# Seven block products in a feed-forward network: all factors of w_in made during the experts, longer load runs, conversion and activation steps staggered

## Chip, cores and metric

The kernel runs on one core of one Trainium2 chip. The metric is the time of one execution on the device in microseconds (us); lower is better.

## The reference

Attention with a threshold, then a mixture of eight experts (each token goes to the one expert with the highest logit), then a feed-forward network with a leaky activation. Only the last two stages are touched:

```
# x: 2304 tokens x 512; e runs over 8 experts, F = 1024
h = np.maximum(x[mask] @ w1[e], 0.0)
out[mask] = gate_w[mask, None] * (h @ w2[e])
# network: w_in 512 x 2048, w_out 2048 x 512, alpha 2048
h = x @ w_in
g = np.maximum(h, 0.0) + alpha * np.minimum(h, 0.0)
return (g @ w_out).astype(np.float32)
```

`w_in` and `w_out` arrive as 64-bit floats. The kernel takes them as pairs of 32-bit words and converts them on the chip.

## The kernel before

Every matrix product is made from operands split into a high half (rounded to fp32r) and a low half (what is left), with three matmuls: high by high, high by low, low by high. ScalarE (ACT) makes the high half, VectorE (DVE) or GpSimd (POOL) subtracts to get the low one. The order of instructions on each engine is the order in which the Python code issues them; every engine runs its own in that order and waits on semaphores. SyncE (SP) issues nearly all DMAs, also in order.

**Experts** (`experts`, L1050 to L1515). 64 steps `g`, eight for each expert `r = g // 8`. In a step, `l1` makes one 128-row piece of the hidden layer (12 matmuls on L1196, as wide as the expert's capacity: 432, 256, 384, 256, 368, 272, 320, 288 tokens), `relu` splits it (L1179, L1180), and `l2` multiplies the piece before by w2 (12 matmuls, L1227 to L1229). `wsplit` prepares a piece of w1 three steps ahead and a piece of w2 two steps ahead: a cast on ACT (L1108), a subtraction on DVE (L1109). Their loads (`wload`, L1095) bring 512 KB for two steps, in a ring of two; those of w1 are cut into 256 columns, so each run in memory is 1 KB.

Beside that, the steps carry other work. `conv` (L1555) turns one piece of w_in into fp32: ACT L1567, DVE L1569, L1571, L1573, L1584, L1585, POOL L1588; one conversion in 3.6 steps. From step 24 on, one entry of the list `early` is taken in each step: for w_in's row blocks 1, 2 and 0, `sums` (L1616: four additions, L1621 to L1624) and seven times `weights` (L1628: cast L1635, subtraction L1636, store L1637 to a DRAM buffer `ws`). From step 31 on, 18 scattered stores of the gate table go out on POOL (L1350). In the last expert, `ahead` fetches the network's first 768 tokens and makes differences and halves of them (`fetch`, `diff`, `split`, L1639 to L1671).

**Network** (`near_network`). Three passes `q` of 768 tokens, each of eight blocks `i` of 256 columns of w_in. Within a block, the first product is not made in eight quarter products but in seven, from sums and differences of the quarters of w_in and of the tokens: `prod` (6 matmuls of 128x384, L1724) in the order 1, 2, 6, 7, 5, 3, 4, into two PSUM banks `ha` and `hb`. `held` copies `ha` out on ACT (L1729). `act` adds it to `hb` on DVE (L1735), makes the two ReLU parts on ACT (L1742, L1743) and joins them on DVE (L1744) in pass 0, or does both on DVE (L1739, L1740) later, and then splits: `gh` on ACT (L1746), `gl` on POOL (L1747). `f2mm` (9 matmuls of 128x512, L1761 to L1763) multiplies by w_out; there are four in a block. So a block has 42 + 36 matmuls on TensorE (PE), the same in each pass.

Pass 0 also converts the fifteen remaining pieces of w_out (`conv` again, with POOL L1591 and L1592), one step of the generator after each product, and makes the factors of w_in's blocks 3 to 7 (`sums` on DVE, `weights` on DVE for two products and on POOL for five). Passes 1 and 2 load the factors from `ws` (L1632). At the end of a pass, `after` prepares the tokens of the next one (`diff` and `split` on DVE).

The program has a second branch for badly spread routing; it is not run here.

Of the kernel before, what the change touches and what calls it, by code (L numbers as in the profile page):

```python
# [44 lines left out]
CVG = {False: [18 * i // 5 for i in range(KF2 + 1)], True: [4 * i for i in range(15)] + [59, 61]}  # L45
# [6 lines left out]
NPRE = 3  # L52
EARLY = 24
AHEAD = 8 * (NE - 1)
# [157 lines left out]
def attn_moe_ffn(ctx: ExitStack, tc, q, k, v, tau, emb, mtau, w1, w2, w_in, w_out, alpha, out):  # L212
# [841 lines left out]
    def experts(CAPS, general, y2):  # L1054
# [7 lines left out]
        sm_p = mpool("sm", bufs=1)  # L1062
        stg_p = mpool("stg", bufs=2)
# [16 lines left out]
        def wload(which, u):  # L1080
# [6 lines left out]
            e = W[r]["e"]  # L1087
            t = stg_p.tile([128, 1024], F32, tag=f"stg{which}", name=f"stg{which}")
# [9 lines left out]
        def wsplit(which, g):  # L1098
# [3 lines left out]
            t = w_p.tile([128, 2, 512], F32R, tag=f"w{which}", name=f"w{which}")  # L1102
            if which == 1:
# [5 lines left out]
            nc.vector.tensor_tensor(t[:, 1], src, t[:, 0].bitcast(F32), op=ALU.subtract)  # L1109
# [378 lines left out]
        for g in range(NE * KF + 1):  # L1488
# [21 lines left out]
            if g >= AHEAD and ahead:  # L1510
                ahead.pop(0)(xt_p)
            if g >= EARLY and early:
                early.pop(0)()
# [10 lines left out]
    def shared(st, general):  # L1524

        y2 = {}
        aw_p = st.enter_context(tc.tile_pool(name="aw", bufs=KF2 if general else NP, side="right", reuse_waits="tile"))
        if general:
            WI = [aw_p.tile([128, 2, DM], F32R, tag="aw", name=f"wi{c}") for c in range(KF2)]
        else:  # L1530
            WA = [aw_p.tile([128, 2, DM], F32, tag="aw", name=f"wa{c}") for c in range(NP)]
# [12 lines left out]
        def cvload():  # L1544
# [5 lines left out]
            if which == 1:  # L1550
                nc.sync.dma_start(flat.rearrange("p (k f) -> p k f", k=KD),
                                  w_in.bitcast(U32)[:, c * 256:(c + 1) * 256].rearrange("(k p) f -> p k f", p=128))
            else:
                nc.sync.dma_start(flat, w_out.bitcast(U32)[c * 128:(c + 1) * 128, :])
            CV[which, c] = flat.rearrange("p (n w) -> p n w", w=2)  # L1555

        def conv():
# [19 lines left out]
            sums = which == 1 and not general  # L1577
            if not sums:
                if c not in WO:
                    WO[c] = aw_p.tile([128, 2, DM], F32R, tag="aw", name=f"wo{c}")  # L1580
                hl = WI[c] if which == 1 else WO[c]
                nc.scalar.copy(hl[:, 0, :], ff)
            yield
# [3 lines left out]
            if sums:  # L1587
                nc.gpsimd.tensor_tensor(WA[c // 2][:, c % 2], ff, rf, op=ALU.add)  # L1588
                yield
                return  # L1590
            nc.gpsimd.tensor_tensor(ff, ff, hl[:, 0, :].bitcast(F32), op=ALU.subtract)  # L1591
            nc.gpsimd.tensor_tensor(hl[:, 1, :], ff, rf, op=ALU.add)  # L1592
            yield
# [430 lines left out]
```

## Time and profile before

| | us |
|---|---|
| median of 3 runs (1078.19 to 1078.75) | 1078.25 |
| the profiled execution | 1081.63 |
| its span, first to last instruction | 1079.8 |
| PE busy, whole span | 984.6 (91%) |
| DVE, ACT, POOL busy | 767.9, 596.3, 587.4 |
| attention and routing | 0 to 358.4 |
| experts | 358.4 to 615.7 |
| network, pass 0 | 615.7 to 796.8 |
| network, pass 1 | 796.8 to 930.3 |
| network, pass 2 and the end | 930.3 to 1079.8 |

The stage limits are the starts of the first matmul of the stage on PE. PE's busy time is modelled at its ends, so it counts short gaps as busy; a stage's length against that of an undisturbed stretch with the same matmuls says more.

### The profile page before, as it was taken

The page shows a single profiled execution, that of the slowest core. Times are in us where ns is not written, and L with a number is a line of the kernel's source. Part 1 is how long each engine was busy: PE and PEld are TensorE (multiplying, and loading weights), DVE is VectorE, ACT ScalarE, POOL GpSimd, SP SyncE. Part 2 cuts the span into 40 slices and gives each one's busy share as a digit, 9 for nine tenths or more (in the row PEclk, how much of TensorE's full clock was granted, in tenths as well). Part 3 has the DMA queues.
Part 4 walks back from the last instruction along what each step waited for, and adds up shares of the span by engine and source line. Part 5 has one row for each costly group of instructions (what it writes and reads, how often), then busy time and mean ns, then how long its engine had stood idle before and what let it go on. Part 6 is the DMA issues. An engine that isn't in the chain of part 4 may idle for free. (4 is left out here: it accounts for less than half of the span.)

```text
span 1079.8 us, 18205 instructions
## 1 busy us (share of the span) xinstructions
PE 984.6 (91%) x6099; PEld 906.2 (84%) x6099; DVE 767.9 (71%) x1474; ACT 596.3 (55%) x1373; POOL 587.4 (54%) x592
## 2 busy tenths in 40 slices
PE   7999999999996999989979768877789999999995
PEld 6999998999996899989979767756678899888994
DVE  7999999999997777798768657766665344644342
ACT  6899898899995455455545354545453222322221
POOL 6989899899995111247631445556534232242233
PEclk8999999999997999999999878898889999999998
DMA  3333547335432858699997354333255344444321
GB/s 91 103 85 90 146 137 237 98 106 155 122 103 100 286 188 263 204 252 242 259 265 224 79 142 137 116 118 126 98 167 173 118 117 142 142 164 118 116 81 62
DMA packets 123015, 161.26 MB, mean 149 GB/s; under 512 B 23304, under 2 KB 80648, under 8 KB 122912
## 3 DMA queue, kind: packets, MB, share of 16 engines
q1 hardware_dynamic: 119312, 150.42, 47.6%
q0 software_dynamic: 3456, 9.46, 2.3%
q8 instruction: 50, 0.82, 0.3%
q14 instruction: 53, 0.43, 0.1%
q10 hardware_dynamic: 144, 0.13, 0.0%
HBM read 108.08 MB, written 43.04 MB: 140 GB/s over the span
## 5 line engine op out<-in xcount | busy, mean ns | idle before, releaser
L1747 POOL TENSOR_TENSOR gl<-c,gh 128x384 fp32r<-128x384 f32 x96 | 102.3, 1067 | 244.3 <-ACT gh L1746 224.9
L1724 PE MATMUL ha<-x,wr 128*128 128x384 f32 x576 | 122.7, 349 | 18.7 <-ACT v L1729 12.4
L1746 ACT CAST gh<-c 128x384 fp32r<-128x384 f32 x96 | 49.3, 513 | 157.5 <-DVE c L1740 122.0
L1724 PEld LDWEIGHTS ha<-x,wr 128*128 128x128 f32 x576 | 105.9, 194 | 31.3 <-ACT v L1729 15.5
L443 POOL TENSOR_TENSOR ptl<-x,pth 128x512 fp32r<-128x512 f32 x97 | 124.8, 1288 | 6.8
L1724 PE MATMUL hb<-x,wr 128*128 128x384 f32 x432 | 97.0, 362 | 27.4 <-DVE c L1735 25.0
L647 DVE SCALAR_TENSOR_TENSOR p<-s,mx,e 128x576 f32<-128x576 f32 x144 | 116.6, 812 | 6.8 <-ACT mx L635 2.9
L1196 PE MATMUL l<-x,w 128*128 128x256 f32 (+6 forms) x744 | 120.0, 310 | 0.0
L1109 DVE TENSOR_TENSOR w<-stg,w 128x512 fp32r<-128x512 f32 x128 | 104.1, 828 | 21.0 <-ACT w L1108 20.3
L1762 PE MATMUL o<-wo,gh 128*128 128x512 f32 x288 | 117.5, 408 | 0.0
L1763 PE MATMUL o<-wo,gl 128*128 128x512 f32 x288 | 116.8, 405 | 0.0
L1761 PE MATMUL o<-wo,gh 128*128 128x512 f32 x288 | 116.5, 405 | 0.0
L631 DVE TENSOR_REDUCE mx<-s 128x1 f32<-128x576 f32 x144 | 108.5, 754 | 8.6 <-PE s L624 5.5
L660 PE MATMUL t<-ident,p 128*128 128x128 f32 (+1 forms) x720 | 112.0, 277 | 2.2 <-ACT x L686 0.9
L1196 PEld LDWEIGHTS l<-x,w 128*128 128x128 f32 x744 | 112.0, 190 | 0.6
L1724 PEld LDWEIGHTS hb<-x,wr 128*128 128x128 f32 x432 | 82.1, 204 | 34.1 <-DVE c L1735 30.5
L640 ACT ACTIVATE e<-s,mx 128x576 f32<-128x576 f32 x144 | 106.3, 739 | 6.6 <-DVE mx L631 6.0
L1588 POOL TENSOR_TENSOR wa<-f,r 128x512 f32<-128x512 f32 x16 | 23.6, 1472 | 137.2 <-DVE r L1585 113.0
L1108 ACT CAST w<-stg 128x512 fp32r<-128x512 f32 x128 | 76.3, 619 | 38.6 <-DMA stg<-in_moe_w_dram 38.6
L1228 PE MATMUL y<-h,w 128*128 128x256 f32 (+6 forms) x256 | 80.7, 315 | 8.7 <-DVE h L1180 8.7
L660 PEld LDWEIGHTS t<-ident,p 128*128 128x128 f32 (+1 forms) x720 | 81.1, 137 | 8.0 <-ACT x L686 2.2
L1227 PE MATMUL y<-h,w 128*128 128x256 f32 (+6 forms) x256 | 82.8, 324 | 5.0 <-ACT yT L1235 3.5
(254 smaller groups left out, 2486.8 us busy)
## 6 DMA issues: line engine op xcount, KB each, us to landing
stg<-in_moe_w_dram SPq DMA_DIRECT2D x64, 512.0 KB
wr<-ws SPq DMA_DIRECT2D x126, 256.0 KB
ws<-wr SPq DMA_DIRECT2D x56, 256.0 KB
kx<-ks SPq DMA_DIRECT2D x60, 144.0 KB
xd<-zt SPq DMA_DIRECT2D x33, 256.0 KB
raw<-in_moe_w_in_dram SPq DMA_DIRECT2D x16, 512.0 KB
raw<-in_moe_w_out_dram SPq DMA_DIRECT2D x16, 512.0 KB
yd<-zt SPq DMA_DIRECT2D x19, 256.0 KB
```

The source lines that it names most:

```text
L443: lambda: nc.gpsimd.tensor_tensor(lo, raw, hi.bitcast(F32), op=ALU.subtract))
L631: nc.vector.tensor_reduce(out=mx[:, 0:1], in_=st["s", t][:, :, 0:288], op=ALU.min, axis=AX.XY)
L640: nc.scalar.activation(e, st["s", t][:, :, 0:288], AF.Exp, bias=st["mx", t][:, 0:1], scale=-1.0)
L647: nc.vector.scalar_tensor_tensor(out=p.rearrange("q (a b) -> q a b", a=2), in0=st["s", t][:, :, 0:288], scalar=st["mx", t][:, 2:3], in1=st ...
L660: nc.tensor.transpose(m[0:w, j * n + i * 128:j * n + (i + 1) * 128], st["p", t][:, c * 128:c * 128 + w], ident)
L1109: nc.vector.tensor_tensor(t[:, 1], src, t[:, 0].bitcast(F32), op=ALU.subtract)
L1196: nc.tensor.matmul(m[:, 0:n], w[:, a, c], st["x"][:, b, c, 0:n], start=(i == 0), stop=(i + 1 == len(terms)))
L1724: nc.tensor.matmul(m, w[:, a, k], x[:, b, k], start=start and n == 0, stop=n + 1 == len(terms), skip_group_check=not start)
L1747: nc.gpsimd.tensor_tensor(gl, c, gh.bitcast(F32), op=ALU.subtract)
L1761: nc.tensor.matmul(m, gh[:, ts], WO[f][:, 0, :], start=(n[0] == 1), stop=False)
L1762: nc.tensor.matmul(m, gh[:, ts], WO[f][:, 1, :], start=False, stop=False)
L1763: nc.tensor.matmul(m, gl[:, ts], WO[f][:, 0, :], start=False, stop=(n[0] == KF2))
```

## The change

1. All 56 factors (eight blocks by seven products) and the eight groups of sums are made during the experts, from step 6.8 on, all on POOL with the cast on ACT, and all are stored to `ws`. Pass 0 loads them from there as passes 1 and 2 do. The converted w_in is now kept for two blocks at a time.
2. w1 is loaded in pieces of 512 columns (1 MB for four steps, a ring of two), w_in in 512 words by 256 rows: runs of 2 KB in memory.
3. From step 7 on, every fourth piece of w2 has its low half made on POOL and not on DVE.
4. In the network, the steps after a product are put off: `join` comes one product later than the ReLU parts, `halves` one later still (`tick`); the generator of a conversion starts every fourth product and several run at once (`cstep`), with the cast a product after the DVE steps and POOL a product after that.
5. In the last expert, the tokens of five of the seven products (1, 2, 6, 7, 5) are split before the network begins, in its last four steps; before, it was three (1, 2, 6). At the end of a pass, differences 1 and 3 go to POOL, and half 6 is made after the addition of product 4, not before it.

```diff
-CVG = {False: [18 * i // 5 for i in range(KF2 + 1)], True: [4 * i for i in range(15)] + [59, 61]}
+CVG = {False: [17 * i // 5 for i in range(KF2 + 1)], True: [4 * i for i in range(15)] + [59, 61]}
...
-NPRE = 3
-EARLY = 24
-AHEAD = 8 * (NE - 1)
+AHEAD = {0: 0, 4: 1, 5: 2, 6: 3, 7: 4}
...
+            if which == 1 and not general:
+                a, b = ((0, 256), (256, 512))[u] if u < 2 else (0, 512)
+                if c % 2 == 0:
+                    STG[1, u] = stg_p.tile([128, KD, 512], F32, tag="stg1", name="stg1")
+                elif u > 1:
+                    return
+                f0 = c // 2 * 512
+                nc.sync.dma_start(STG[1, u - c % 2][:, :, a:b],
+                                  w1[bass.ds(e, 1), :, f0 + a:f0 + b].rearrange("o (k p) f -> p (o k) f", p=128))
+                return
...
+            eng = nc.gpsimd if not general and which == 2 and g % 4 == 1 and g > 8 else nc.vector
...
-            if g >= EARLY and early:
-                early.pop(0)()
+            while early and early[0][0] <= g:
+                early.pop(0)[1]()
...
+        def factor(i, p, eng):
+
+            t, flat, home = wtile(i, p)
+            src = SUM[i][p]
+            hi, lo = (t[:, x].rearrange("p (k j) -> p k j", k=2) for x in range(2))
+            nc.scalar.copy(hi, src)
+            eng.tensor_tensor(lo, src, hi.bitcast(F32), op=ALU.subtract)
             nc.sync.dma_start(home, flat)
+
+        def weights(q, i, p):
+
+            WT[q, i, p], flat, home = wtile(i, p)
+            nc.sync.dma_start(flat, home)
...
-        for i in (*range(1, NPRE), 0):
-            y2["early"] += [lambda i=i: sums(i, nc.gpsimd)] + [lambda i=i, p=p: weights(0, i, p, nc.gpsimd, True) for p in PROD]
+        G = nc.gpsimd
+        for i in range(NP):
+            g0 = 6.8 * i + 6.8
+            y2["early"].append((g0, lambda i=i: sums(i, G)))
+            y2["early"] += [(g0 + 0.8 * x, lambda i=i, p=p: factor(i, p, G)) for x, p in enumerate(PROD)]
+        y2["early"] += [(61.5 + 0.3 * x, lambda p=p: weights(0, 0, p)) for x, p in enumerate(PROD)]
...
+        def tick():
+            for x in pend:
+                x.pop(0)()
+            pend[:] = [x for x in pend if x] + fresh
+            fresh.clear()
...
+        def cstep():
+
+            if count[0] % 4 == 0 and count[1] < KF2 - 1:
+                live.append(conv())
+                count[1] += 1
+            count[0] += 1
+            for x in list(live):
+                if next(x, 1):
+                    live.remove(x)
...
-                for f, x in {6: [(split, 1)], 7: [(split, 2)], 5: [(diff, 1), (diff, 3)], 3: [(diff, 2), (split, 6)],
-                             4: [(diff, 4)]}.get(p, ()):
-                    f(x, V)
+                for f, x, e in {6: [(split, 1, V)], 7: [(split, 2, V)], 5: [(diff, 1, P)], 3: [(diff, 2, V), (diff, 3, P)],
+                                4: [(split, 6, V), (diff, 4, V)]}.get(p, ()):
+                    f(x, e)
...
-                if q == 0 and NPRE <= i + 1 < NP:
-                    sums(i + 1, V)
...
-                def step(p, m, start=False):
-                    prod(q, i, p, m, start)
-                    next(stages, None)
+                def step(p):
+                    tick()
+                    after(q, i, p)
+                    cstep()
```

POOL during the experts, about step 36 before the change, rows that only repeat left out here and below (`wa` is a converted piece of w_in, `sum` the sums, `wr` a factor, `pd` the gate table):

```order
L1588 TENSOR_TENSOR wa_5885<-f,r 128x512
L1636 TENSOR_TENSOR wr<-wa_5883,wr 128x256
L1350 DMA pd<-idg,ysl_i 2304x2
L1636 TENSOR_TENSOR wr<-sum,wr 128x256
L1588 TENSOR_TENSOR wa_5886<-f,r 128x512
```

and after it, between two conversions at about step 13:

```order
L1611 TENSOR_TENSOR wa<-f,r 128x512
L1646 TENSOR_TENSOR sum<-wa 128x256
L1647 TENSOR_TENSOR sum<-sum,wa 128x256
L1648 TENSOR_TENSOR sum<-wa 128x256
L1649 TENSOR_TENSOR sum<-wa,sum 128x256
L1662 TENSOR_TENSOR wr<-wa,wr 128x256
L1133 TENSOR_TENSOR w_6771<-stg_6574,w_6771 128x512
L1662 TENSOR_TENSOR wr<-sum,wr 128x256 x3
L1611 TENSOR_TENSOR wa<-f,r 128x512
```

The sums, the factors and the low half of a w2 piece (L1133) now stand together on POOL, all through the experts.

POOL in pass 0, in a middle block, before (`gl` is the low half of the activation, `wo` a piece of w_out):

```order
L1747 TENSOR_TENSOR gl<-c,gh 128x384
L1636 TENSOR_TENSOR wr<-wa_5886,wr 128x256
L1636 TENSOR_TENSOR wr<-sum,wr 128x256
L1591 TENSOR_TENSOR f<-f,wo_9939 128x512
L1592 TENSOR_TENSOR wo_9939<-f,r 128x512
```

and after:

```order
L1790 TENSOR_TENSOR gl<-c,gh 128x384 x2
L1616 TENSOR_TENSOR f<-f,wo_9271 128x512
L1617 TENSOR_TENSOR wo_9271<-f,r 128x512
L1790 TENSOR_TENSOR gl<-c,gh 128x384
L1616 TENSOR_TENSOR f<-f,wo_9272 128x512
```

The factors are gone from it; only activations and conversions are left.

ACT in pass 0, from the first copy of a block on, before (`v`, `w`, `d` are copies of `ha`, `u` and `c` the ReLU parts):

```order
L1729 COPY v<-ha 128x384
L1635 CAST wr<-wa_5888 128x256
L1742 ACTIVATE u<-c 128x384
L1743 ACTIVATE c<-c 128x384
L1746 CAST gh<-c 128x384
L1567 ACTIVATE f<-raw 128x512
L1729 COPY w<-ha 128x384
L1582 CAST wo_10313<-f 128x512
L1729 COPY d<-ha 128x384
```

and after:

```order
L1764 COPY v<-ha 128x384
L1789 CAST gh<-c 128x384
L1777 ACTIVATE u<-c 128x384
L1778 ACTIVATE c<-c 128x384
L1614 CAST wo_9277<-f 128x512
L1764 COPY w<-ha 128x384
L1594 ACTIVATE f<-raw 128x512
L1764 COPY d<-ha 128x384
```

Before, the cast `gh` stood right behind the ReLU parts that it needs joined on DVE; now the cast behind the first copy belongs to an earlier product.

## Rows read from the trace of the kernel before

**Rows 1.** Busy time by stage: stretch, length, five engines, PE clock, DMA share, GB/s.

```profile
core 0: us, PE busy (x) PEld busy (x) DVE busy (x) ACT busy (x) POOL busy (x), PEclk, DMA share, GB/s
358.40:615.70 257.30, 243.64 (x1613) 236.33 (x1614) 199.54 (x339) 132.45 (x292) 93.06 (x76) 0.99 0.80 226
615.70:796.80 181.10, 142.62 (x599) 120.47 (x599) 121.01 (x165) 87.11 (x188) 101.71 (x87) 0.87 0.42 136
796.80:930.30 133.50, 128.96 (x625) 114.98 (x623) 63.11 (x103) 36.68 (x70) 39.82 (x38) 0.97 0.44 133
```

**Rows 2.** The same view, by blocks of the network.

```profile
635.90:655.90 20.00, 17.42 (x80) 15.42 (x79) 13.43 (x17) 9.31 (x20) 10.20 (x8) 0.91 0.37 131
655.90:775.50 119.60, 94.83 (x391) 79.09 (x390) 81.75 (x115) 56.97 (x128) 71.03 (x63) 0.87 0.34 117
775.50:796.80 21.30, 17.72 (x80) 14.87 (x79) 13.80 (x19) 10.37 (x21) 11.98 (x10) 0.92 0.62 209
796.80:820.60 23.80, 19.26 (x80) 16.30 (x79) 16.03 (x24) 11.26 (x19) 10.02 (x10) 0.86 0.37 117
820.60:836.30 15.70, 15.70 (x80) 14.11 (x79) 6.07 (x12) 3.49 (x7) 5.53 (x6) 1.00 0.48 158
930.30:951.60 21.30, 18.16 (x80) 15.47 (x80) 14.86 (x23) 10.11 (x17) 9.94 (x10) 0.92 0.43 138
```

**Rows 3.** Who waited for whom in pass 0, 615.7 to 796.8: total us, times, longest.

```profile
ACT gh L1746 <- DVE c L1744: 33.0, 30, 2.9
PE hb L1724 <- DVE c L1735: 19.8, 13, 3.2
PE ha L1724 <- ACT v L1729: 12.4, 5, 4.4
```

**Rows 4.** Timeline, single operations: start, length in us, engine, line, operation.

```profile
628.14 1.26 POOL L1591 TENSOR_TENSOR f<-f,wo 128x512 f32<-128x512 f32 x1
629.47 1.27 POOL L1592 TENSOR_TENSOR wo<-f,r 128x512 fp32r<-128x512 f32 x1
788.73 1.02 POOL L1747 TENSOR_TENSOR gl<-c,gh 128x384 fp32r<-128x384 f32 x1 [1.04 <-ACT gh L1746]
632.43 0.42 DVE L1569 TENSOR_SCALAR f<-f 128x512 f32<-128x512 f32 x1
548.65 0.69 DVE L1573 SCALAR_TENSOR_TENSOR f<-raw,f 128x512 uint32<-128x512 uint32 x1
631.90 0.62 DVE L1744 SCALAR_TENSOR_TENSOR c<-u,na,c 128x384 f32<-128x384 f32 x1 [1.15 <-ACT c L1743]
```

**Rows 5.** Timeline, the same DVE subtraction alone and beside POOL.

```profile
539.66 0.69 DVE L1109 TENSOR_TENSOR w<-stg,w 128x512 fp32r<-128x512 f32 x1 [0.31 <-ACT w L1108]
...
597.82 2.18 POOL L1665 TENSOR_TENSOR raw<-raw 128x768 f32<-128x768 f32 x1
598.22 2.33 DVE L1109 TENSOR_TENSOR w<-stg,w 128x512 fp32r<-128x512 f32 x1
```

**Rows 6.** Busy time by stretches of the experts, columns as in the first group.

```profile
395.20:420.10 24.90, 24.90 (x206) 24.78 (x205) 22.63 (x43) 15.51 (x35) 3.02 (x2) 1.00 0.79 250
516.40:544.40 28.00, 27.29 (x206) 26.13 (x204) 22.42 (x35) 15.25 (x36) 20.70 (x19) 1.00 1.05 252
544.40:581.30 36.90, 31.05 (x206) 29.48 (x205) 25.16 (x44) 18.57 (x41) 6.99 (x6) 1.00 0.91 251
...
534.00:544.00 10.00, 10.00 (x78) 9.53 (x77) 8.57 (x15) 4.23 (x10) 6.65 (x6) 1.00 1.12 206
```

**Rows 7.** POOL's groups during the experts: busy us, mean ns, idle before.

```profile
L1588 POOL TENSOR_TENSOR wa<-f,r 128x512 f32<-128x512 f32 x16 | 23.6, 1472 | 137.2 <-DVE r L1585 113.0 <-ACT h L1179 20.8 <-DMA ws<-wr 3.4
L1350 POOL DMA_INDIRECT pd<-idg,ysl_i x18 | 21.7, 1204 | 2.9 <-issue 2.4 <-DMA ws<-wr 0.2
L1636 POOL TENSOR_TENSOR wr<-sum,wr 128x256 fp32r<-128x256 f32 x12 | 11.5, 960 | 6.7 <-ACT wr L1635 6.7
L1623 POOL TENSOR_TENSOR sum<-wa 128x256 f32<-128x256 f32 x3 | 2.9, 967 | 0.0
```

More of the change, by code (lines that the diff above doesn't have):

```diff
@@ L1062, in experts @@
         sm_p = mpool("sm", bufs=1)
+        if not general:
+            y2["wa"] = mpool("wa", bufs=1)
         stg_p = mpool("stg", bufs=2)
@@ L1102, in wsplit @@
             t = w_p.tile([128, 2, 512], F32R, tag=f"w{which}", name=f"w{which}")
+            eng = nc.gpsimd if not general and which == 2 and g % 4 == 1 and g > 8 else nc.vector
+            if which == 1 and not general:
+                t = t.rearrange("p x (k f) -> p x k f", k=KD)
+                v, j = u // 2 * 2, g % 4
+                src = STG[1, v][:, :, j * 128:(j + 1) * 128]
+                nc.scalar.copy(t[:, 0], src)
+                nc.vector.tensor_tensor(t[:, 1], src, t[:, 0].bitcast(F32), op=ALU.subtract)
+                RING[which, g] = t
+                if g == 1:
+                    wload(1, 2)
+                elif j == 3:
+                    STG.pop((1, v))
+                    wload(1, v + 4)
+                return
             if which == 1:
@@ L1586, in conv @@
             cvload()
-            if sums:
+            yield
+            if which == 1 and not general:
+                if c % 2 == 0:
+                    WA[c // 2] = y2["wa"].tile([128, 2, DM], F32, tag="wa", name="wa", bufs=2)
                 nc.gpsimd.tensor_tensor(WA[c // 2][:, c % 2], ff, rf, op=ALU.add)
-                yield
                 return
+            hl = WI[c] if which == 1 else WO[c]
+            nc.scalar.copy(hl[:, 0, :], ff)
+            yield
             nc.gpsimd.tensor_tensor(ff, ff, hl[:, 0, :].bitcast(F32), op=ALU.subtract)
             nc.gpsimd.tensor_tensor(hl[:, 1, :], ff, rf, op=ALU.add)
-            yield
         y2["cvload"], y2["conv"] = cvload, conv
@@ L1625, in sums @@
[L1625 to L1633 removed]
+            s = y2["wa"].tile([128, 4, 256], F32, tag="sum", name="sum", bufs=1)
@@ L1712, in near_network @@
         NQ = NT // NB
-        sums, weights, fetch, split, diff = (y2[x] for x in ("sums", "weights", "fetch", "split", "diff"))
+        weights, fetch, split, diff = (y2[x] for x in ("weights", "fetch", "split", "diff"))
         conv, cvload, rawtile = y2["conv"], y2["cvload"], y2["rawtile"]
```

146 lines of the change are left out of this document (75 added, 71 removed).

## The prediction

> **What bounds the kernel now.** I read the busy times by stage first. The chain that ended last is no help here: it holds only the final scatters. In the experts PE is busy 243.6 of 257.3 us, in pass 0 only 142.6 of 181.1, in pass 1 129.0 of 133.5 [rows 1]. All passes have the same matmuls, so the blocks of the network show what pass 0 could be: an undisturbed block takes 15.7 us at a granted clock of 1.00 [rows 2], eight of them 125.6 us. Pass 0 has 55 us more than that. The reader should see three levels in [rows 2]: 15.7 us with PE alone; 20.0 us in the second block, which has conversions of w_out but makes no factors; and 119.6 us for the five blocks after it, 23.9 each, where factors are made too. The first blocks of passes 1 and 2 stand out as well, with 23.8 and 21.3. Last, the waits of pass 0 [rows 3]: PE waits 19.8 us for DVE's addition to free `hb` and 12.4 us for ACT's copy of `ha`, and ACT waits 33.0 us, in 30 pieces, for DVE's join before it can cast `gh`. So PE is held up by engines that are themselves stuck behind a step of the same product. The granted clock of 0.86 to 0.91 there is a mixture of the two levels, 1.2 and 2.4 GHz, that follows PE's gaps.
>
> The experts are nearer to a bound. Where steps are short (256 tokens), a stretch without POOL work takes 24.9 us for eight steps with DVE busy 22.6; the stretch with 272 tokens, POOL busy 20.7 and DVE 22.4 takes 28.0 where the same pace per column would give 26.5 (24.9 x 272 / 256); and in the one of 320 tokens, 36.9 us, PE is busy 31.1 only, behind a stretch where the DMA share was 1.12 with 206 GB/s [rows 6].
>
> **Term 1, factors leave pass 0: -19.6 us.** Blocks 3 to 7 lose sums, casts, subtractions and stores, and become like block 2: 119.6 - 5 x 20.0 = 19.6 [rows 2]. What replaces them is a load of 256 KB per product, as passes 1 and 2 have it without a loss (158 GB/s at a share of 0.48 in the 15.7 us block).
>
> **Term 2, staggered steps: -20 us.** What is left is at most 20.0 - 15.7 = 4.3 us a block, at least nothing. An operation that reads two tiles of SBUF on DVE and one on POOL do not run at once: the subtraction on L1109 takes 0.69 us alone and 2.33 us when it starts in the middle of a POOL operation, which itself runs 2.18 us [rows 5]. So I add up what excludes each other in a block after the change: on POOL four `gl` of 1.02 and two conversions of 1.26 + 1.27, 9.1 us; on DVE four joins of 0.62 and two conversions of 0.42, 0.43 (the next of the same kind) and 0.69, 5.6 us [rows 4]. That is 14.7 us in a block that PE can do in 15.7: it does not bind by itself, but leaves little room. I take six tenths of the 4.3 us as gained, so 17.4 us a block, because the waits that hold PE are those that the new order pulls apart: 19.8 + 12.4 us [rows 3] of the 38.5 in which PE is idle. The first block keeps two token splits (18.5 us where 181.1 - 20.0 - 119.6 - 21.3 = 20.2 were), the last keeps the next pass's (18.7 where 21.3 were). Pass 0 becomes 18.5 + 6 x 17.4 + 18.7 = 141.6 us, 39.5 less than now; 19.6 of it is term 1.
>
> The Trainium skill states this exclusion too (SBUF — State Buffer, section Who interferes with whom): VectorE and GpSimd share a pair of ports, whoever issues first has it for the whole instruction, and the other is blocked, not slowed. The trace agrees, with 2.33 us for 0.69. A rule that speaks against the change stands in Perfetto Trace Analysis, section Optimizing Scalar/DVE Operations, of the same skill: as the two share that port, moving operations between them might not help. By that rule the fourteen w2 halves given to POOL cost more exclusive time than they save, and the third case below becomes likelier; the rows do not show the moved operation.
>
> **Term 3, ends of passes: -3.5 us.** The two first blocks have 8.1 and 5.6 us over 15.7 [rows 2]. In both, DVE's addition for product 4 stands behind difference 2 and split 6; the split now comes after it, but difference 2 waits for difference 1, which is now made on the slower POOL. Bounds: a small loss of 2 us and a gain of 8; I take 3.5, a quarter of the excess, since the splits themselves stay.
>
> **Term 4, experts: +10 us.** Moved in: five more sums of four operations and 32 more factors on POOL, 14 w2 halves on POOL instead of DVE, 39 more transfers of 256 KB on SP's queue (32 stores, 7 loads at the end). POOL's new work at the means of [rows 7]: 20 x 0.97 + 32 x 0.96 + 14 x 1.47 (as L1588, same size) = 71 us, on top of 93.1 [rows 1], so 164 of 257. Before, 113.0 us of POOL's time went in waiting for DVE's conversion [rows 7], so POOL has room on average. What counts is the short experts, where PE does not cover it. The 256-token stretch without POOL work should become like the 272-token one: 24.9 to 28 us. The 272-token stretch has the gate stores (18 of 1.20 us, most of them there) beside more factors: +2.5 us. The others, longer or already loaded, +1 together. DMA: 226 GB/s over 257.3 us are 58.1 MB [rows 1]; 39 x 0.26 MB and one early piece of w_out (0.5 MB) make 68.8. The 516 to 544 stretch moved 252 GB/s at a share of 1.05, so about 240 at full share; the 256-token one 250 at 0.79, so 316 [rows 6]. At those, 68.8 MB need 287 or 218 us: between them lies the length of the stage, and loads will come late at times. Against that stand the longer runs (the 15.7 us block with 2 KB runs alone gives 158 / 0.48 = 329 GB/s, 4% over 316) and w1 loaded a step of 1 MB ahead. I add 3.5 us for late loads. Sum 3.1 + 2.5 + 1 + 3.5 = 10. Every factor store makes SP wait for POOL, and the loads of w2 queue behind it; that is in these 3.5 us. Bounds: nothing lost, or +30 (all 68.8 MB at 240 GB/s, 287 us).
>
> The new splits in the last expert, two more on DVE and one on POOL, fall in its last steps, which have no w1 pieces left to prepare; I cost them at nothing, and 2 us more if DVE's `h` waits behind them.
>
> **Sum:** -39.5 - 3.5 + 10 = -33. The profiled execution's own 1081.6 would become 1048.6; the median of the runs is 3.4 us lower, so I forecast 1078.3 - 33 = **1045 us**.
>
> **Rivals.**
> First, forecast: 1045, its own range 1033 to 1058. Chance 0.52.
> Second, PE bound: the stagger takes all of it. Pass 0 is 8 x 15.7 + 4 us for the splits = 130, -51; the ends give 5, the experts lose 2 because w1's longer lead pays for the stores. 1078.3 - 54 = 1024. For it: 14.7 us of exclusive work is less than 15.7. Against: each engine runs in order, and 94% filled without a gap is rare. Chance 0.17.
> Third, the stagger does not do what it says: POOL and DVE exclude each other as before, a block stays at 20.0 us, the ends give nothing, the experts +10: 1078.3 - 19.6 + 10 = 1069, and to 1085 where w2 pieces come late on POOL. For it: the block of 20.0 us has exclusive work of 14.7 us already, so order, not amount, must give the rest. Against: 33.0 us of ACT waiting that the new order removes. Chance 0.20.
> Fourth, slower: the DMA queue binds the experts. If 68.8 MB go at the 206 GB/s of the stretch with a share of 1.12 [rows 6], where stores of yT and factors met, the stage lasts 334 us, +77, and the total is 1078 - 43 + 77 = 1112. It decides from a rate below 229 GB/s (68.8 MB in 257.3 + 43 us). For it: 2.3 times as many factor stores. Against: the stretch lasted 10 us, and longer ones held 251. Chance 0.11.
>
> **How the numbers follow.** About 0.2% (2 us) is what a measurement of this kernel can tell from no change. The first two cases are faster. Of the third, 0.14 is faster, 0.04 within that bound, 0.02 slower; of the fourth, 0.10 slower and 0.01 the same. So faster 0.83, same 0.05, slower 0.12. The range goes from 1018 (which leaves out 0.02 of the second case) to 1070 (which leaves out the upper third of the third, 0.07, and the fourth, 0.11).
>
> **What would show it.** Pass 0 should be near 142 us with middle blocks of 17 to 18 us and a clock over 0.9; ACT's wait for the join should fall from 33.0 us to under 10. The experts should last near 267 us, longer in the short experts than now, with POOL over 150 us busy. The first blocks of passes 1 and 2 should lose 1 to 3 us each; the others stay at 15.7. I am wrong if middle blocks stay at 20 (term 2), if the experts grow by over 25 us (term 4), or if DMA waits appear in pass 0.

## Result and profile after

| | before | after |
|---|---|---|
| median, us | 1078.5 (4 runs, 1078.2 to 1081.0) | 1050.7 (4 runs, 1048.4 to 1056.5) |
| profiled execution, us | 1081.6 | 1048.4 |
| experts | 257.3 | 267.1 |
| network, pass 0 | 181.1 | 143.8 |
| network, pass 1 | 133.5 | 130.9 |
| network, pass 2 and the end | 149.5 | 146.3 |

The ratio of the times is 0.9745, with a 95% interval of 0.9703 to 0.9788. The medians are 27.8 us apart, and the interval gives 23 to 32 us. The profiled executions are 33.2 us apart, against a forecast of 33; but the one after is the fastest of its four, and the one before took longer than all four in the table. So the stage lengths, which come from these two executions, overstate the gain by about 5 us in all.

Busy time by stage after the change (columns as in [rows 1]):

```profile
358.40:625.50 267.10, 249.50 (x1612) 241.92 (x1613) 207.63 (x325) 143.87 (x329) 162.65 (x146) 0.96 0.88 258
625.50:769.30 143.80, 128.21 (x599) 112.17 (x598) 104.58 (x135) 72.66 (x150) 81.33 (x62) 0.95 0.54 169
769.30:900.20 130.90, 128.10 (x625) 114.20 (x624) 65.64 (x100) 35.97 (x71) 45.48 (x42) 0.99 0.45 137
```

Set against [rows 1], the experts are 9.8 us longer and POOL works 162.7 us in them, not 93.1. Pass 0 is 37.3 us shorter; the same 599 matmuls keep PE busy 128.2 us instead of 142.6, because the clock is at its higher level for more of the time (granted clock 0.95, was 0.87), and the rest of the gain is waiting that is gone.

The same view for some blocks of the network after the change, to be read beside [rows 2]: blocks 2, 5 and 6 of pass 0, the first blocks of passes 1 and 2.

```profile
658.60:674.30 15.70, 15.70 (x80) 14.12 (x79) 12.34 (x18) 9.29 (x20) 10.42 (x8) 1.00 0.55 185
708.80:730.80 22.00, 18.78 (x80) 16.42 (x78) 14.11 (x17) 10.17 (x22) 9.55 (x8) 0.84 0.45 159
730.80:749.30 18.50, 16.20 (x79) 14.04 (x78) 14.29 (x17) 8.72 (x19) 10.04 (x8) 1.00 0.43 141
769.30:790.30 21.00, 18.20 (x79) 15.30 (x78) 15.23 (x23) 11.36 (x20) 10.85 (x10) 0.92 0.43 136
900.20:917.90 17.70, 16.12 (x79) 13.96 (x79) 15.02 (x23) 9.51 (x16) 9.38 (x9) 1.00 0.50 160
```

Pass 0 is uneven: its blocks take 15.5, 17.6, 15.7, 16.9, 17.6, 22.0, 18.5 and 20.0 us. Block 2 runs at PE's own pace with conversions beside it; the last three are furthest from it. The first blocks of the later passes are 2.8 and 3.6 us shorter.

Who waited for whom in pass 0 after the change (total us, times, longest; rows of [rows 3] are the counterparts):

```profile
ACT u L1777 <- DVE c L1773: 41.0, 21, 5.7
...
PE hb L1759 <- DVE c L1773: 11.2, 6, 3.2
...
ACT gh L1789 <- DVE c L1785: 4.4, 2, 2.2
```

ACT's wait for the join fell from 33.0 to 4.4 us, and PE's wait for the addition from 19.8 to 11.2. ACT now waits for that addition instead, 41.0 us. Most of this is idle time and costs nothing; the longest pieces, of over 5 us, are where PE waits too.

Busy time in the experts 1, 3, 5 and 7 (256, 256, 272 and 288 tokens) after the change:

```profile
395.20:420.10 24.90, 24.90 (x205) 24.77 (x205) 23.30 (x37) 15.95 (x37) 16.91 (x15) 1.00 0.79 270
...
454.20:480.20 26.00, 24.88 (x205) 24.68 (x205) 24.58 (x45) 15.40 (x36) 16.69 (x18) 1.00 1.00 265
...
518.30:550.80 32.50, 29.93 (x206) 28.78 (x206) 25.40 (x37) 17.64 (x42) 25.99 (x25) 0.89 1.01 252
...
586.70:625.50 38.80, 31.33 (x206) 30.20 (x205) 19.51 (x25) 16.88 (x38) 26.62 (x20) 0.87 0.67 194
```

The short expert 1 takes 24.9 us as before [rows 6], now with 16.9 us of POOL work in it where there were 3.0. The losses are late: expert 4 (38.1 us, was 34.1), 5 (32.5, was 28.0) and 7 (38.8, was 34.3). What ended waits in the experts after the change:

```profile
ACT w L1132 <- DMA stg<-in_moe_w_dram: 40.2, 15, 9.2
DVE h L1204 <- ACT h L1203: 29.5, 28, 2.6
DVE w L1133 <- ACT w L1132: 15.4, 5, 9.0
```

The first of these before the change, for the loads of w1 and w2 together:

```profile
ACT w L1108 <- DMA stg<-in_moe_w_dram: 31.5, 19, 4.0
```

ACT stands 40.2 us at the cast of a w2 piece whose load has not landed, once for 9.2 us in the last expert. The ReLU of a step is queued behind that cast on ACT, and PE waits for the ReLU. Loads were late before the change too (31.5 us), but in shorter pieces.

### The profile page after: what moved, and what is told of

Same layout as the page of the kernel before. It is cut to its first block, busy times and chain, and to the rows that moved or that the text cites. A ratio compares the mean times of both kernels' runs of the same rounds, so it can differ in the third digit from the quotient of the medians.

```text
span 1046.5 us, 18304 instructions
## 1 busy us (share of the span) xinstructions
PE 972.2 (93%) x6099; PEld 900.1 (86%) x6099; DVE 765.9 (73%) x1426; ACT 590.6 (56%) x1373; POOL 642.4 (61%) x640
## 4 chain that ended last, share of the span: by engine, by line
PE 53%; DVE 16%; issue 8%; DMA 8%; ACT 7%; POOL 7%; SPq 0%; POOLq 0%; ACTq 0%; DVEq 0%
PE ha L1759 7%; PE hb L1759 6%; PE s L622 5%; PE o L1819 5%; PE o L1818 5%; PE o L1817 5%; PE t L658 4%; DMA stg<-in_moe_w_dram 4%; PE l L1220 4%; DVE p L645 2%; DVE mx L629 2%; PE v L702 2%; PE m L721 2%; PE v L703 2%; PE y L1252 2%
## 5 line engine op out<-in xcount | busy, mean ns | idle before, releaser
L1790 POOL TENSOR_TENSOR gl<-c,gh 128x384 fp32r<-128x384 f32 x96 | 106.7, 1114 | 221.6 <-ACT gh L1789 134.2
L1759 PE MATMUL ha<-x,wr 128*128 128x384 f32 x576 | 118.4, 341 | 4.4 <-ACT c L1778 2.8
L1818 PE MATMUL o<-wo,gh 128*128 128x512 f32 x288 | 115.2, 400 | 0.0
L1817 PE MATMUL o<-wo,gh 128*128 128x512 f32 x288 | 114.1, 396 | 0.0
L1759 PE MATMUL hb<-x,wr 128*128 128x384 f32 x432 | 91.1, 347 | 15.3 <-DVE c L1773 15.3
L1251 PE MATMUL y<-h,w 128*128 128x256 f32 (+6 forms) x256 | 84.9, 332 | 11.2 <-ACT h L1203 7.3
L1759 PEld LDWEIGHTS hb<-x,wr 128*128 128x128 f32 x432 | 78.3, 194 | 18.7 <-DVE c L1773 18.1
L1252 PE MATMUL y<-h,w 128*128 128x256 f32 (+6 forms) x256 | 82.7, 323 | 6.4 <-DVE h L1204 6.2
L622 PE MATMUL s<-ks,qs 128*128 128x288 f32 x256 | 82.7, 338 | 2.9 <-ACT qs L529 1.4
L1253 PE MATMUL y<-h,w 128*128 128x256 f32 (+6 forms) x256 | 81.5, 318 | 0.0
L1773 DVE TENSOR_TENSOR c<-hb,d 128x384 f32<-128x384 f32 x24 | 13.4, 557 | 91.4 <-ACT d L1764 91.4
```

What stands on the lines that cost most here:

```text
L622: nc.tensor.matmul(s[:, hf, 0:288], lt, st[nm, a][:, hf * 288:(hf + 1) * 288], start=(j == 0 and x == 0), stop=(j == n - 1 and x == 1))
L1759: nc.tensor.matmul(m, w[:, a, k], x[:, b, k], start=start and n == 0, stop=n + 1 == len(terms), skip_group_check=not start)
L1790: nc.gpsimd.tensor_tensor(gl, c, gh.bitcast(F32), op=ALU.subtract)
L1817: nc.tensor.matmul(m, gh[:, ts], WO[f][:, 0, :], start=(n[0] == 1), stop=False)
L1818: nc.tensor.matmul(m, gh[:, ts], WO[f][:, 1, :], start=False, stop=False)
```

## Experiments

Times are medians; the ratio is to the kernel before, run on the same chip. Stage lengths are those of each kernel's profiled execution.

| kernel | us | ratio, 95% interval | experts | pass 0 |
|---|---|---|---|---|
| changed kernel | 1050.7 | 0.9745 [0.9703, 0.9788] | 267.1 | 143.8 |
| activation at once | 1076.2 | 0.9967 [0.9947, 0.9986] | 263.9 | 162.9 |
| before, activation staggered | 1056.1 | 0.9778 [0.9754, 0.9802] | 252.5 | 163.2 |
| w2 on DVE | 1053.1 | 0.9737 [0.9700, 0.9774] | 268.1 | 145.6 |
| each store twice | 1195.7 | 1.1045 [1.1013, 1.1078] | 413.2 | 144.2 |
| copy to a second buffer | 1072.8 | 0.9933 [0.9905, 0.9962] | 293.9 | 141.5 |
| w1 in halves, 1 KB runs | 1046.7 | 0.9686 [0.9663, 0.9710] | 265.2 | 142.2 |
| third buffer for w2 | 1035.2 | 0.9581 [0.9562, 0.9599] | 254.2 | 142.2 |
| third buffer, other splits | 1037.4 | 0.9604 [0.9574, 0.9633] | 251.5 | 144.6 |
| old order of a conversion | 1037.6 | 0.9596 [0.9567, 0.9625] | 269.2 | 131.1 |
| POOL's pair earlier | 1039.6 | 0.9607 [0.9574, 0.9640] | 270.7 | 133.6 |
| third buffer and old order | 1024.9 | 0.9488 [0.9464, 0.9511] | 255.9 | 130.2 |
| the same, w1 in halves | 1026.9 | 0.9501 [0.9476, 0.9526] | 258.1 | 130.4 |

### What the staggered activation is worth

Undone in the changed kernel:

```diff
-            if q:
-                join()
-                fresh.append([halves])
-            else:
-                first()
-                fresh.append([join, halves])
+            if not q:
+                first()
+            join()
+            halves()
```

> The changed kernel with the activation's join and halves issued at once behind the ReLU parts, in all passes; conversions and factors as in the changed kernel. Theory A, the two parts of pass 0 are about equal: pass 0 goes from 143.8 back to 158 to 163 us, middle blocks near 20, total 1064 to 1070. Rival, the factors' leaving gave all of it: pass 0 stays within 3 us of 143.8 and the total at 1051. Passes 1 and 2 stay the same but for their first blocks by either.

Pass 0 goes from 143.8 to 162.9 us, and the first blocks of passes 1 and 2 from 21.0 and 17.7 to 23.4 and 24.5. The waits in pass 0 of this kernel:

```profile
DVE c L1785 <- ACT c L1778: 35.6, 29, 2.3
ACT gh L1789 <- DVE c L1785: 27.4, 30, 1.8
...
PE hb L1759 <- DVE c L1773: 22.0, 9, 3.7
```

The thirty waits of ACT for the join are back (27.4 us), those of DVE for the ReLU parts with them, and PE waits 22.0 us for the addition. The opposite experiment puts the stagger alone (the same three steps, put off in the same way, with one buffer more for `u` and for `c`) into the kernel before, where factors are still made in pass 0:

```diff
+            def first():
...
+            def join():
...
+            def halves():
...
+            if q:
+                join()
+                fresh.append([halves])
+            else:
+                first()
+                fresh.append([join, halves])
```

> The kernel before with the activation staggered alone: factors and conversions stay where they were. If the waits of the activation are independent of the factors: pass 0 from 181 to 159 to 166 us, first blocks of the later passes 2 to 6 us shorter each, median 1050 to 1060. Rival: with the factors in place POOL and DVE are full, so pass 0 stays over 172 and the median over 1066.

Pass 0 takes 163.2 us, and the first blocks of passes 1 and 2 take 19.1 and 19.7 us, 4.7 and 1.6 less. So pass 0 takes 181.1 us with neither part, 163.2 with the stagger alone, 162.9 with everything but it, 143.8 with both. Either part, the stagger or the rest of the change, is worth 18 to 19 us, whether the other is there or not. The rest is more than the factors' leaving: it holds the new order of the conversions and the earlier token splits as well. The rival (POOL and DVE too full for it to help while factors are made) is excluded.

### What the experts lose

Three reasons were open: POOL's low halves of w2 come late, the added transfers fill the DMA queues, or loads are asked for too late. First, w2's low halves back on DVE:

```diff
-            eng = nc.gpsimd if not general and which == 2 and g % 4 == 1 and g > 8 else nc.vector
+            eng = nc.vector
```

> The changed kernel with all low halves of w2 on DVE again (14 fewer subtractions on POOL, 14 more on DVE). Theory A, late loads come from order: SP's queue waits 23.9 us for POOL's w2 subtractions before it can reuse their staging tile, and 62.6 us for POOL's factors; with this piece gone the experts lose some of those waits, 267.1 to about 261 to 264 us, the rest unchanged, total about 1046. Theory B, late loads come from bytes: same bytes, so the experts stay at 265 to 269. Theory C, DVE is the tighter engine in the short experts: the experts get longer, 270 or more.

1053.1 us against 1050.7, with intervals that lie on each other; the experts last 268.1 us. Moving fourteen subtractions to POOL neither gains nor costs anything that can be measured. SP's waits for those subtractions, 23.9 us in the changed kernel's profile, are gone, though SP now waits 24.9 us and not 12.2 for DVE at the same loads (L1105, for `w` and `h`). So about half of that wait was removed, and the stage is no shorter.

Then more bytes, by issuing every factor's store twice:

```diff
             nc.sync.dma_start(home, flat)
+            nc.sync.dma_start(home, flat)
```

> The changed kernel with each of the 56 factor stores issued twice (same data to the same place): 14.7 MB more in the experts, with 56 more entries in SP's queue and nothing more on POOL, ACT or DVE. Theory A, order: SP's extra entry waits for nothing new, so the experts grow only by a few us, to 268 to 275. Theory B, bytes: about 70 MB become 84; at the 258 GB/s that the stage moves that is 57 us more to move, so the experts grow by 30 us or more, to about 300 to 325. Pass 0 within 3 us by both.

The experts grow to 413 us, but this tells nothing of bytes. SP's waits in this kernel, from 395 to 770 us:

```profile
SPq L1664 <- DMA ws<-wr: 244.1, 55, 8.8
```

The second store goes to the same place as the first, so SP waits until the first has landed, 4.4 us each, 55 times; every load behind it on SP's queue waits as well. The copy was therefore sent to a second DRAM buffer, so that nothing waits for it:

```diff
+    wsb = dram.tile([NP, len(PROD), 128, DM], F32, name="wsb")
...
             nc.sync.dma_start(home, flat)
+            nc.sync.dma_start(wsb[i, PROD.index(p)], flat)
```

> The changed kernel with each factor stored a second time into a buffer of its own, so that the second store waits for nothing of the first (in the run with double stores to one place, SP stood 244 us for the first store's landing, so it did not weigh the bytes). 14.7 MB more, 56 more entries on SP's queue. Theory A, lead and order decide: the rate rises above 258 GB/s and the experts grow by 5 to 15 us, to 272 to 282. Theory B, bytes bind at about 258 GB/s: the experts grow by 40 us or more, to 305 to 325.

The experts take 293.9 us, between the two ranges. Their row, and ACT's wait for weights in them:

```profile
358.40:652.30 293.90, 256.39 (x1613) 246.93 (x1613) 196.35 (x325) 142.52 (x328) 158.13 (x146) 0.93 0.94 284
```

```profile
ACT w L1133 <- DMA stg<-in_moe_w_dram: 82.9, 16, 10.8
```

At 284 GB/s this is 83.5 MB, 14.6 MB more than the changed kernel's 68.9 (258 GB/s over 267.1 us), as 56 stores of 0.26 MB should be. So the queues could carry 284 GB/s, and the changed kernel's 258 were not their limit. More bytes do cost time, through loads that come later still.

Length of runs and size of a transfer, with w1's 1 MB load cut into two of 512 KB and 1 KB runs, asked for at the same time:

```diff
-                a, b = ((0, 256), (256, 512))[u] if u < 2 else (0, 512)
+                a, b = ((0, 256), (256, 512))[u % 2]
...
-                elif u > 1:
-                    return
...
                     wload(1, v + 4)
+                    wload(1, v + 5)
```

> The changed kernel with w1 loaded in runs of 1 KB again, two loads of 512 KB in place of one of 1 MB, into the same two staging tiles and issued at the same point, so that only run length and the number of loads change. If run length matters, the DMA share rises by about 4% at the same bytes and the experts grow by 3 to 10 us (270 to 277). If the longer lead was all that part 2 gave, the experts stay at 265 to 269 and the total near 1051.

1046.7 us: 2 KB runs are no gain over 1 KB runs here. If anything the halves are better by 4 us.

Last the moment at which w2 is asked for: a third buffer, so that each load is issued one pair of steps earlier, with the same transfers:

```diff
-            t = stg_p.tile([128, 1024], F32, tag=f"stg{which}", name=f"stg{which}")
+            t = stg_p.tile([128, 1024], F32, tag=f"stg{which}", name=f"stg{which}", bufs=3 if which == 2 and not general else 2)
...
-                wload(which, u + 2)
+                wload(which, u + (3 if which == 2 and not general else 2))
...
+        if not general:
+            wload(2, 2)
```

> The changed kernel with three staging tiles for w2 instead of two, each load issued two steps earlier. Theory A, order: ACT's 48 us of waiting for w1 and w2 loads falls under 20 and the experts go from 267.1 to 256 to 260 us, total about 1042. Theory B, bytes: an earlier issue does not move more bytes; ACT's waits fall a little at first and the experts stay at 264 to 268.

1035.2 us. The experts' row in this kernel:

```profile
358.40:612.60 254.20, 243.31 (x1612) 236.10 (x1613) 215.50 (x326) 144.11 (x330) 168.04 (x146) 0.99 0.91 271
```

271 GB/s over 254.2 us are 68.9 MB, the same bytes, carried in 12.9 us less. ACT's wait for w2's loads, 40.2 us in the changed kernel, is gone; 2.0 us for a load of w1 are left. All of POOL's added work and all 56 stores are still there, SP still waits 60.6 us for POOL's factors (62.6 in the changed kernel), and the stage as a whole is as short as before the change. So what the stage lost, it lost through w2 loads that landed too late, and a longer lead hides this. What made them late, the added bytes or SP's waits for POOL's factors in front of them, is not separated; the run with the second buffer shows that added bytes without added POOL work can. The last expert, with its five splits, takes 34.1 us here (34.3 before the change).

The sum hides two opposite differences, though. The experts 5 and 6 (272 and 320 tokens) of this kernel, to be read beside [rows 6], and PE's wait in expert 5:

```profile
516.60:548.20 31.60, 28.61 (x205) 27.34 (x204) 28.54 (x37) 18.11 (x42) 28.04 (x25) 0.95 1.04 271
548.20:578.70 30.50, 30.50 (x206) 29.66 (x206) 27.50 (x41) 17.58 (x42) 18.97 (x18) 0.99 1.03 288
```

```profile
PE y L1252 <- DVE h L1204: 3.0, 1, 3.0
```

Expert 5 is still 3.6 us longer than before the change, without a wait for w2's loads: POOL is busy 28.0 us in it and not 20.7, DVE 28.5 and not 22.4, and PE waits for DVE. Expert 6 is 6.4 us shorter than before the change, where ACT waited 12.4 us for loads. The run with w2's halves on DVE fits this: with two buffers its expert 5 takes 29.8 us, with DVE busy 23.1, where the changed kernel takes 32.5; its expert 6 takes 42.3 us, with one wait of 10.3 for a load. So the third buffer also gives back what late loads cost before the change, and POOL's work most likely does cost something in one short expert. What a third buffer would give the kernel before was not tried.

With three buffers it was tried whether the last expert gains when two of its five splits come a step later:

```diff
-AHEAD = {0: 0, 4: 1, 5: 2, 6: 3, 7: 4}
+AHEAD = {0: 0, 4: 1, 5: 2, 7: 3}
...
-            ((diff, 3, G), (diff, 2, G)), ((split, 6, V), (split, 7, V)),
-            ((diff, 4, G), (split, 5, V)))]
+            ((diff, 3, G), (diff, 2, G)),
+            ((split, 6, V), (split, 7, V), (diff, 4, G), (split, 5, V)))]
```

> The kernel with three staging tiles for w2 and, in the last expert, token splits 6 and 7 issued one step later, behind the last ReLU on ACT. Theory: in the last expert PE waits 3.8 us for ACT's ReLU, which stands behind the cast of split 6, which waits 6.2 us for POOL's difference 2; moved behind it, the last expert goes from 34.1 to 29 to 31 us, total 1031 to 1033. Rival: the splits then arrive too late for product 6 of the first block, which grows from 14.1 by as much, total 1035.

1037.4 us, no difference to 1035.2. The last expert loses 2.1 us (34.1 to 32.0) and the first block of pass 0 takes them back (14.1 to 16.3), with 4.1 us of PE's waiting for a factor's load. This moved the time and saved none.

### What pass 0 still loses

The change also put a conversion into another order: cast after the last two DVE operations, POOL's two operations one product after that. With the old order (cast ahead of the last two, POOL's two in their step):

```diff
+            if which == 2 or general:
+                hl = WI[c] if which == 1 else WO[c]
+                nc.scalar.copy(hl[:, 0, :], ff)
+                yield
             nc.vector.tensor_scalar(out=r, in0=f, scalar1=0xFF800000, scalar2=None, op0=ALU.bitwise_and)
...
             cvload()
-            yield
             if which == 1 and not general:
+                yield
...
-            hl = WI[c] if which == 1 else WO[c]
-            nc.scalar.copy(hl[:, 0, :], ff)
-            yield
             nc.gpsimd.tensor_tensor(ff, ff, hl[:, 0, :].bitcast(F32), op=ALU.subtract)
             nc.gpsimd.tensor_tensor(hl[:, 1, :], ff, rf, op=ALU.add)
+            yield
```

> The changed kernel with the steps of a w_out conversion in the old order (cast on ACT one product earlier, before the last two DVE steps; POOL's two operations in the same product as these). The activation stays staggered. Theory A, the activation's stagger gives nearly all of the difference between 143.8 and 162.9 us of pass 0 and the conversion's little: pass 0 at 144 to 150. Rival, the conversion's steps matter as much: pass 0 at 155 or more, with ACT waiting over 15 us for DVE before the cast.

Both expectations missed, to the good side: pass 0 falls to 131.1 us and the median to 1037.6. So the new order costs 13 us. PE's wait for the addition in pass 0 of this kernel, 11.2 us in the changed one:

```profile
PE hb L1761 <- DVE c L1775: 2.4, 4, 1.3
```

Two things had moved in that edit, the cast and POOL's pair. The next kernel keeps the new order of the operations and only drops the pause ahead of the cast, so that POOL's pair comes one product earlier:

```diff
             cvload()
-            yield
             if which == 1 and not general:
+                yield
```

> The changed kernel with a conversion's cast in the same step as the last two DVE operations and POOL's two operations so one product earlier, the order of the operations unchanged. Theory A (POOL's two stood on top of the next conversion's three on DVE): pass 0 falls from 143.8 to 130 to 135 us, the median to 1037 to 1042. Theory B (what helped was the cast ahead of DVE's pair): pass 0 stays at 140 to 147, the median at 1047 to 1053.

Pass 0 takes 133.6 us, the median is 1039.6, as theory A said. A similar place in the two kernels shows how. In the changed kernel, the timeline of DVE, POOL and PE around the addition that PE waits for in block 6 (start, length, engine, line, operation, idle time before and what ended it):

```profile
731.73 0.77 DVE L1596 TENSOR_SCALAR f<-f 128x512 f32<-128x512 f32 x1 [1.66 <-ACT f L1594]
732.53 1.40 DVE L1598 TENSOR_SCALAR f<-f 128x512 uint32<-128x512 uint32 x1
733.97 1.67 DVE L1600 SCALAR_TENSOR_TENSOR f<-raw,f 128x512 uint32<-128x512 uint32 x1
735.56 1.36 DVE L1785 SCALAR_TENSOR_TENSOR c<-u,na,c 128x384 f32<-128x384 f32 x1
...
737.90 0.55 DVE L1773 TENSOR_TENSOR c<-hb,v 128x384 f32<-128x384 f32 x1
...
731.20 1.02 POOL L1790 TENSOR_TENSOR gl<-c,gh 128x384 fp32r<-128x384 f32 x1 [7.41 <-ACT gh L1789]
732.18 1.48 POOL L1616 TENSOR_TENSOR f<-f,wo 128x512 f32<-128x512 f32 x1
733.73 1.36 POOL L1617 TENSOR_TENSOR wo<-f,r 128x512 fp32r<-128x512 f32 x1
735.05 1.46 POOL L1790 TENSOR_TENSOR gl<-c,gh 128x384 fp32r<-128x384 f32 x1
...
738.50 1.31 PE L1759 MATMUL hb<-x,wr 128*128 128x384 f32 x6 [2.29 <-DVE c L1773]
```

The same addition in the kernel with POOL's pair earlier:

```profile
731.05 0.98 DVE L1596 TENSOR_SCALAR f<-f 128x512 f32<-128x512 f32 x1 [1.44 <-ACT f L1594]
732.07 0.43 DVE L1598 TENSOR_SCALAR f<-f 128x512 uint32<-128x512 uint32 x1
732.53 1.39 DVE L1600 SCALAR_TENSOR_TENSOR f<-raw,f 128x512 uint32<-128x512 uint32 x1
733.85 0.61 DVE L1785 SCALAR_TENSOR_TENSOR c<-u,na,c 128x384 f32<-128x384 f32 x1
...
735.43 0.55 DVE L1773 TENSOR_TENSOR c<-hb,v 128x384 f32<-128x384 f32 x1
...
729.27 1.50 POOL L1617 TENSOR_TENSOR wo<-f,r 128x512 fp32r<-128x512 f32 x1
730.73 1.02 POOL L1790 TENSOR_TENSOR gl<-c,gh 128x384 fp32r<-128x384 f32 x1
732.35 1.02 POOL L1790 TENSOR_TENSOR gl<-c,gh 128x384 fp32r<-128x384 f32 x1 [0.60 <-ACT gh L1789]
...
736.04 1.31 PE L1759 MATMUL hb<-x,wr 128*128 128x384 f32 x6 [0.51 <-DVE c L1773]
```

In the changed kernel POOL works without a gap from 731.2 to 736.5, and four DVE operations ahead of the addition take 0.77, 1.40, 1.67 and 1.36 us beside it, 5.2 in all. In the other kernel POOL's pair is over before them (two `gl` still fall beside them); they take 3.4, and PE waits 0.51 us and not 2.29. PE's next six matmuls take 1.31 us in both, so only the wait differs here. This is only half of theory A, though: over the whole pass the three operations of a conversion take DVE 46.4 us in the changed kernel (13.2 + 15.2 + 18.0) and still 42.1 here (10.9 + 13.2 + 18.0). So most of the overlap is not gone. That it moved to conversions without an urgent addition behind them is shown at this one place; for the rest of the pass it is inferred from PE's wait for the addition, which falls from 11.2 to 5.9 us. PE's waits in pass 0 fall from 15.5 to 10.9 us, and its busy time from 128.2 to 122.6 us, since the granted clock is 1.00 over the whole pass (blocks 1, 5 and 7 of the changed kernel have 0.90, 0.84 and 0.91); together that is the 10.2 us. In block 5 of the changed kernel both are seen at once:

```profile
717.40 2.29 PE L1759 MATMUL hb<-x,wr 128*128 128x384 f32 x6 [3.22 <-DVE c L1773]
727.68 1.20 PE L1759 MATMUL hb<-x,wr 128*128 128x384 f32 x6
```

After 3.22 us of waiting six matmuls take 2.29 us, and six of the same size 10 us later 1.20 (granted clock 0.50 from 719 to 722 us, so 1.2 GHz, and 1.00 from 725 on).

### Both repairs together

The third buffer for w2 and the old order of a conversion:

> The third buffer for w2's loads and the old order of a conversion together. If the two losses lie in different stages and add up: 1035.2 + 1037.6 - 1050.7 = 1022 us, experts 252 to 256 us, pass 0 130 to 134. Rival: the two overlap (a conversion early in pass 0 depends on loads that the deeper ring pushes back), then pass 0 stays over 137 and the time lies at 1027 to 1033.

1024.9 us, 2.5% less than the changed kernel and 5.1% less than before; the two add up within 3 us. Experts and pass 0 of this kernel, and ACT's wait for weights in the experts:

```profile
357.80:613.70 255.90, 243.66 (x1613) 236.19 (x1614) 214.47 (x325) 143.97 (x329) 167.84 (x146) 0.99 0.91 270
613.70:743.90 130.20, 123.05 (x599) 107.45 (x599) 101.63 (x133) 72.81 (x149) 84.36 (x62) 1.00 0.60 188
```

```profile
ACT w L1132 <- DMA stg<-in_moe_w_dram: 4.2, 2, 2.1
```

The 40.2 us of waiting for weights are 4.2, and pass 0 runs at a granted clock of 1.00. With w1 in halves of 1 KB runs on top (the diff of that experiment added to these two):

> As the kernel with both edits, and w1 loaded in two halves of 1 KB runs. If the 4 us that the halves gave alone (1046.7 against 1050.7) came from w2's loads standing less long behind 1 MB of w1, the third buffer has taken that gain already: 1021 to 1024, no difference to the kernel with both. Rival: shorter transfers help by themselves: 1016 to 1020.

1026.9 us, no difference. What the halves may have gained alone, the third buffer has taken.

## Why the prediction was right, and where it was not

The forecast was 1045 us, the median is 1050.7. The medians differ by 27.8 us where the sum said 33; that the two profiled executions differ by 33.2 is luck of the draw. The total agrees better than its parts.

**Term 1, factors leave pass 0 (-19.6).** Right in sign; its size is not measured by itself. All of the change but the stagger is worth 18.2 us (181.1 to 162.9, without the stagger) or 19.4 (163.2 to 143.8, with it), which looks like the term. But the five blocks that the term was summed from fall by 14.1 us without the stagger (119.7 to 105.6) and by 17.0 with it (107.7 to 90.7); the first block, with its splits moved, gives 4 to 5 more. And both differences carry the new order of the conversions. With the stagger and the old order these five blocks take 81.9 us, so the rest of the change is worth 25.8 us there against the kernel before with the stagger. How much of this is the factors alone stays open. The term's cover held: PE waits for no load in pass 0 of the changed kernel.

**Term 2, staggered steps (-20).** Terms 1 and 2 together said 141.6 us for pass 0, measured are 143.8: the first block 15.5 (18.5 said), the next six 18.1 on average (17.4), from 15.7 to 22.0, the last 20.0 (18.7). The mechanism is shown: ACT's wait for the join went to 4.4 us (forecast: under 10), and the stagger of the activation alone gives 18 to 19 us. But "six tenths of the 4.3 us" is a right size for a wrong reason. I took what remains over 15.7 us for the stagger's limit. The runs show 13 us of it to be a cost of the same change, the new order of a conversion, which puts POOL's pair on DVE's operations ahead of an addition. I had added up how long the two exclude each other in a block (14.7 us), and did not look at which operation of DVE the overlap falls on. Without it, pass 0 is 130.2 to 131.1 us: the 130 of the second rival, "the stagger takes all of it", is what this code can do.

The Trainium skill's rule that VectorE and GpSimd block each other (SBUF — State Buffer, section Who interferes with whom) agrees with the timeline above: the same operation on L1598 takes 1.40 us when POOL is in the middle of an operation at its start, and 0.43 when it is not. Another rule of the Trainium skill, that moving operations between these two might not help (Perfetto Trace Analysis, section Optimizing Scalar/DVE Operations), fits the w2 halves: 1053.1 us with them on DVE, 1050.7 on POOL, no difference.

**Term 3, ends of passes (-3.5).** Right in sign, wrong in its cause: the first blocks lose 2.8 and 3.6 us, 6.4 in all, but the kernel before with the stagger alone, its splits and differences where they were, loses 4.7 and 1.6, which is 6.3. With the splits moved and no stagger they take 23.4 and 24.5 us, together no less than before. So the moved split and differences, on which the term rested, gave nothing on balance; the stagger, which the term did not count, gave it all. The size is known to some 2 us only: the first block of pass 2 takes 17.7 to 19.5 us in kernels that have the same code there.

**Term 4, experts (+10).** Measured +9.8, with POOL busy 162.7 us where 164 were worked out, but the split of the ten is wrong. The step "the 256-token stretch without POOL work should become like the 272-token one: 24.9 to 28" failed: it takes 24.9 us with 16.9 us of POOL work, and the other short one 26.0 (28.5 before). So the 3.1 were not there. The 2.5 for the 272-token stretch were about right: it is still 2.4 to 3.6 us longer in the four kernels with the third buffer. The 3.5 for late loads were far too low: the third buffer gives back 12.9 us, some of which was lost to late loads before the change already. The row that misled was the 272-token stretch in [rows 6], 28.0 us with much POOL work beside it, read as if that work alone were the reason. The same stretch had a DMA share of 1.05, which was named and not followed; ACT waits 8.5 us for weight loads in it. The estimate of "240 at full share" was too low as well: in the changed kernel the expert at a share of 1.00 moves 265 GB/s, and the kernel with the second buffer 284 over the whole stage. So the fourth rival's condition, under 229 GB/s, was far off. The counts had a slip: the kernel before makes 21 factors in the experts, so 35 were moved in and not 32, with 42 transfers and not 39, and both kernels load two pieces of w_out there. By the same means that gives 167 us of POOL work and 69.1 MB; measured are 162.7 and 68.9.

The splits in the last expert, costed at nothing: right for the total. That expert grew by 4.5 us, but with three buffers and the same splits it takes 34.1 us, as before. Two of the splits cost 2.1 us there, as the run that moved them shows, but moving them costs the first block of pass 0 as much.

One caution: the experts of two kernels with the same code there took 257.3 us (before) and 252.5 (before, with the stagger), and four with the changed kernel's code there 263.9 to 270.7. So a difference of 5 us in this stage between single profiles carries little. The conclusions above rest on two groups of kernels: 251.5 to 258.1 us in the four with a third buffer, 263.9 to 270.7 in six without it, the two with added stores aside. Expert 5 takes 30.4 to 31.6 us in the four with a third buffer, 28.0 and 27.7 in the two kernels before.

Four things were not tried and stay open: what keeps the first block of pass 1 at 22.5 us in the fastest kernel, against 15.7 undisturbed; whether a still longer lead of the loads would give more; what a third buffer gives the kernel before; and what the factors' leaving is worth by itself.

## What to carry over

When a change adds transfers to an in-order queue, first ask how early each load behind them is issued, and give the loads another buffer; that was worth 13 us here at the same bytes. When steps of two engines that block each other are moved by a product, look at which operation stands behind the overlap: a collision ahead of an operation that PE waits for costs the wait and can cost the clock after it (block 5 here, not block 6), while most of the stretched time can stay without harm (42.1 us of it in the pass of 133.6 us). A total that agrees proves no term of it; undo the parts one by one.

## What was not expected of the hardware

- Where the program lets a second store of 256 KB wait for the first to land at the same place in DRAM, SP stood 4.4 us each time (244.1 us in 55 waits), and every load behind it on SP waited too.
- The core's DMA queues moved 284 GB/s over 294 us with loads, stores and gathers mixed, after 226 in the kernel before.
- Loads with runs of 1 KB were no slower than those with 2 KB (1046.7 against 1050.7 us).
- DVE operations of one input are also stretched beside POOL: from 0.43 to 1.40 us on L1598. POOL is stretched too, from 1.02 to 1.46 us on L1790.
